# How the row maxima of a softmax are turned: by blocks on VectorE, or on TensorE at another place

## The chip, the cores and the metric

The kernel runs on one core of one Trainium2 chip. The metric is the device time of one execution in microseconds. Five engines work beside each other: TensorE (PE in the profile, with its weight loads as PEld), VectorE (DVE), ScalarE (ACT), GpSimd (POOL) and SyncE (SP), which here only issues DMAs.

## What is computed

One transformer block on 2048 rows of width 512: a modulated layer norm, attention with 32 heads of width 16, an output projection, a second modulated norm and a gated feed-forward of width 1792. The part around the change is the softmax of the attention:

```python
qkv = (x @ wqkv).reshape(B, S, 3, H, Dh).transpose(2, 0, 3, 1, 4)
q, k, v = qkv[0], qkv[1], qkv[2]
scores = jnp.einsum("bhqd,bhkd->bhqk", q, k) * Dh ** -0.5
p = _softmax(scores, axis=-1)
o = jnp.einsum("bhqk,bhkd->bhqd", p, v)
```

All of it is in fp32; products that need more than one pass of the narrower type split an operand into a high and a low part.

## The kernel before

**Units and steps.** The attention is cut into 32 units: 4 chunks of 512 queries by 8 groups of 4 heads. A unit has 16 steps (one per 128 keys), a step has four pairs (one per head). A pair is two matmuls that share the array, each on one half of its rows: the score of this step (`score`, L506, keys by queries, followed on ACT by the exponential, L508), and one product for the row maximum of a later unit (`max_one`, L479, queries by keys, followed on DVE by a reduce over 512 keys, L481). The maxima run some 20 steps ahead of the scores (`LEAD` = 21). The value products (`pv_step`, L521) use all 128 rows and 32 columns a head; they come in halves of a step.

**Where the maxima go.** The scores are computed with keys on the partitions, so the maximum of a query must be subtracted along the free axis. It is therefore appended to the queries as two more rows (`KR` = 48, and the next) of the operand `qop`, the high part of -max and the remainder, against two rows of ones in the keys. But the maxima lie with queries on the partitions, 128 x 16 values for a unit. `max_rows` (L483) reduces the four parts of each maximum on DVE (L486), negates them on ACT (L498), and turns them on TensorE by three products with a unit matrix (L491 to L493): the high part into one row, the remainder into the other. ACT copies the result out (L495), and two DMAs on SP put it into `qop` (L497).

**The order.** It is written by hand. `after(i)` runs behind step i and starts `max_rows` for unit u behind step 16u-6. `max_rows` does its reduce at once and puts five small jobs into `side`; `pair_of` takes one of them behind each pair. The third is the negation, the fifth is the turn on TensorE with its copy and DMAs. So the turn stands among the pairs.

**Plain and filled steps.** In `plain` three pairs are followed by one or two halves of value products (`HALVES`), and that is all TensorE does; four banks of the accumulator take maxima in turn, three take scores. In `filled` two steps (eight pairs) form a group: between the pairs stand matmuls of the projection or the feed-forward of the chunk before (L719, "filler", up to three yields of two matmuls behind a pair), and behind the eighth pair come `hook` (the DVE work of the filler that has ended) and four halves of value products. Three banks take maxima, two take scores. Filler of a gate-up job takes two groups, that of a down job one. The first filled step is 147, 275 or 403 (`STARTS`); the steps of a chunk are 8 filled, 12 plain (36 in the last), then filled for gate-up and down jobs, with 3 plain ones near the end. The maxima end 20 steps before the scores do; the filled groups behind that point have scores alone, with another order of banks (`ALONE`).

Of the kernel before, what the change touches and what calls it, by code (L numbers as in the profile page):

```python
# [9 lines left out]
F32 = mybir.dt.float32  # L10
F32R = mybir.dt.float32r
# [3 lines left out]
ALU = mybir.AluOpType  # L15
AX = mybir.AxisListType
# [3 lines left out]
P = 128  # L20
# [18 lines left out]
KR = 48  # L39
# [62 lines left out]
def block_kernel(ctx, tc, x, wqkv, wo, w_gate, w_up, w_down, c, w_mod, out):  # L102
    nc = tc.nc
# [18 lines left out]
    four, bank, single = Turn(0, 1, 2, 3), Turn(4, 5, 6), Turn(7)  # L122
# [326 lines left out]
    pb = ctx.enter_context(tc.tile_pool(name="pb", bufs=2, reuse_waits="tile"))  # L449
# [33 lines left out]
    def max_rows(u):  # L483

        m = pb.tile([P, 16], F32, name="m", tag="m")
        nc.vector.tensor_reduce(m, mx.pop(u).rearrange("p b s t f -> p (b s t) f"), op=ALU.max, axis=AX.X)  # L486
        nm = pb.tile([P, 16], F32R, name="nm", tag="nm")

        def rows():
            pr = bank("pr")[0:16, 0:2 * P]  # L490
            nc.tensor.matmul(pr[:, 0:P], nm.bitcast(F32), ident, start=True, stop=True)  # L491
            nc.tensor.matmul(pr[:, P:2 * P], m, minus, start=True, stop=False)  # L492
            nc.tensor.matmul(pr[:, P:2 * P], nm.bitcast(F32), minus, start=False, stop=True)  # L493
            mr = pb.tile([16, 2, P], F32R, name="mr", tag="mr", bufs=1)
            nc.scalar.copy(mr, pr.rearrange("p (r q) -> p r q", r=2))  # L495
            for r in range(2):
                nc.sync.dma_start(qop[u][KR + r:KR + r + 65:64].bitcast(F32), mr[:, r, :].bitcast(F32))  # L497
        side.extend([lambda: None, lambda: None, lambda: nc.scalar.mul(nm, m, -1.0), lambda: None, rows])  # L498

    def score(i, h):  # L500
        u, kt = divmod(i, 16)
# [73 lines left out]
    def split_weights():  # L575

        def raw(src, k):
            t = tile_mid().bitcast(F32)
            nc.gpsimd.dma_start(t.rearrange("p e c -> p (e c)").rearrange("p (k c) -> p k c", k=k), src)
            return t  # L580

        def parts(hi, lo, t):
            nc.gpsimd.tensor_copy(hi, t)
            nc.gpsimd.tensor_sub(lo, t, hi.bitcast(F32))

        def store(dst, w):
            nc.gpsimd.dma_start(dst, w.bitcast(F32))

        def cols(m):
            return slice(m * FG * P, (m + 1) * FG * P)  # L590

        srcs = [(wod[:, 2 * k:2 * k + 2, :], 2) for k in range(NK // 2)]
        for m in range(NF // FG):
            srcs += [(wgd[:, :, cols(m)], NK), (wud[:, :, cols(m)], NK), (wdd[:, m * FG:(m + 1) * FG, :], FG)]
        ahead = [raw(*srcs.pop(0)) for _ in range(2)]
        yield

        def following():
            if srcs:
                ahead.append(raw(*srcs.pop(0)))  # L600
            return ahead.pop(0)

        for k in range(NK // 2):
            t = following()
            nc.gpsimd.tensor_mul(t, t, ga_bc[:, None, :].to_broadcast([P, 2, D]))
            w = tile_gu()
            parts(as_wo(w)[:, 0], as_wo(w)[:, 1], t)
            store(wo_dr[k], as_wo(w))
            yield
        for m in range(NF // FG):  # L610
            ws = [tile_gu() for _ in range(FG)]
            for e in range(2):
                t = following()
                src = t.rearrange("p e c -> p (e c)").rearrange("p (k f c) -> p f k c", k=NK, f=FG)
                for f in range(FG):
                    parts(ws[f][:, 2 * e], ws[f][:, 2 * e + 1], src[:, f])
                    if e:
                        store(gu_dr[m * FG + f], ws[f])
                yield
            t = following()  # L620
            nc.gpsimd.tensor_mul(t, t, gb_bc[:, None, :].to_broadcast([P, FG, D]))
            w = tile_wd()
            parts(w[:, 0], w[:, 1], t)
            store(wd_dr[m], w)
            yield

    class Chunk:
# [42 lines left out]
        def rows(self, t):  # L670
            return self.nt[t // 2][:, t % 2, :]
# [139 lines left out]
    side = []  # L811
# [53 lines left out]
    at(UG - 2, lambda: chunks[0].load_wo())  # L865

    weights2 = split_weights()

    def after(i):
        nonlocal pf  # L870
        for f in due.pop(i, []):
            f()
        j = i + LEAD
        if j % 16 == 15 and j < n:
            max_rows(j // 16)
        if i == -2:
            run(late)
            sm.finish()
            es_a0.close()
            pf = ctx.enter_context(tc.tile_pool(name="pf", bufs=1, side="right", reuse_waits="tile"))  # L880
            kop[2] = pf.tile([P, 2, S], F32R, name="kop2")
            ones_rows(2)
            load_k(2)
            load_q(2)
        if 0 <= i < UG and i % 16 in (3, 5, 8):
            next(weights2, None)

    for i in range(-LEAD, -1):
# [7 lines left out]
        while side:  # L896
            side.pop(0)()

    halves = [(i, half) for i in range(n) for half in range(2)]
    done, ended, owed = 0, 0, 0  # L900
    three = Turn(0, 1, 2)
# [12 lines left out]
    def pvs(most, by_halves):  # L914

        nonlocal owed
        if by_halves:
            most, owed = most + owed, 0
        while most and halves and 4 * halves[0][0] + 8 <= done:
            i, half = halves.pop(0)  # L920
            pv_step(i, half)
            most -= 1
            if i % 16 == 15 and half:
                close_unit(i // 16, done // 4 - 1)
                if by_halves:
                    break
        if by_halves and most and halves and 4 * halves[0][0] + 8 <= done:
            owed = most

    def end_steps():  # L930
        nonlocal ended
        while ended < done // 4:
            after(ended - 1)
            ended += 1

    def plain(steps, tails=()):

        nonlocal four, bank
        assert steps % WIN == 0 and done % 4 == 0
        four, bank = Turn(0, 1, 2, 3), Turn(4, 5, 6)  # L940
        for w in range(4 * steps // WIN):
            for _ in range(WIN):
                pair_of()
            if w >= 4 * steps // WIN - len(tails):
                tails[w - 4 * steps // WIN](four())
            pvs((HALVES[(w - 2) % 4] if done > 8 else 0) + (w == 4 * steps // WIN - 1), True)
            end_steps()

    def filled(places, work):

        nonlocal four, bank
        four, bank = three, Turn(4, 5)
        if done >= 4 * n - 4 * (LEAD - 1):
            places, bank = ALONE.get(places, places), Turn(4, 5, 0, 1, 5, 0, 4, 1)
        for r in range(len(places)):
            pair_of()
            take(work, places[r])
            if r % 4 == 3:
                end_steps()
        hook()  # L960
        pvs(6, False)

    def two_of(u):
        return [kop[u % 3][:, e, :].rearrange("p (k c) -> p k c", k=NK) for e in range(2)]
# [102 lines left out]
```

## Time and profile before

| | |
|---|---|
| time, median of 3 runs | 1880.32 us (1879.69 to 1880.54) |
| span of the profiled execution, first to last instruction | 1875.6 us |
| median less span | 4.7 us |
| PE busy | 1846.7 us, 98% of the span |
| DVE busy | 1541.8 us, 82% |
| ACT busy | 1252.4 us, 67% |
| POOL busy | 415.3 us, 22% |
| granted TensorE clock, mean | 0.999 |

The span belongs to one execution on which the profiler was on; what that execution took beside its span is not listed, so times of whole runs are compared with times of whole runs. Busy times of PE are not its load: matmuls are pipelined, and one that waits behind another in the array counts as busy. In a row of a group the two numbers behind the bar are the busy time of the group (us) and the mean duration of one instruction (ns), then the idle time of the engine just before them and what ended it. In the timeline the columns are the start and the duration in us, engine, line, operation, names, shapes and count, with an idle time before the instruction in brackets. In the table of windows each engine has its busy time and, in brackets, its number of instructions, in the order PE, PEld, DVE, ACT, POOL, and then the granted clock, the DMA share and the GB/s.

### The profile page before, as it was taken

Reading aid. Unit: us, or ns where it says so; the run is one execution under the profiler, and the core shown is the slowest. Engines: PE = TensorE matmul, PEld = TensorE weight load, DVE = VectorE, ACT = ScalarE, POOL = GpSimd, SP = SyncE. Lnnn points to the kernel's source line nnn. Section 1 sums busy time; section 2 is a strip of 40 time slices with the busy share of each in tenths; the row PEclk is TensorE's granted clock in tenths of the full one; section 3 lists DMA queues with packets and bytes.
Section 4 is the critical chain, followed back from the end, with each engine's and each line's share of the span. In section 5 each row is a group of like instructions: output and inputs, shape, how many; then the busy total and the mean of one; then the engine's idle time right before and its main releaser. Section 6 shows DMA issues by size and latency. Waiting matters only on the chain.

```text
span 1875.6 us, 41002 instructions
## 1 busy us (share of the span) xinstructions
PE 1846.7 (98%) x16996; PEld 1160.4 (62%) x16996; DVE 1541.8 (82%) x2558; ACT 1252.4 (67%) x2406; POOL 415.3 (22%) x498
## 2 busy tenths in 40 slices
PE   7999999999999999999999999999999999999999
PEld 5766444444455766666555667666554566667887
DVE  5548999999999888888999888889999988831643
ACT  4221888888887766777777776677878877674211
POOL 3000454456323211111133111111123011030200
PEclk9999999999999999999999999999999999999999
DMA  8855677766843534554454454453643446243642
GB/s 286 292 198 142 174 183 178 201 167 190 211 86 78 145 102 124 144 124 90 107 124 116 108 127 131 121 122 78 159 86 56 108 92 156 86 159 119 249 180 110
DMA packets 78854, 267.62 MB, mean 143 GB/s; under 512 B 17364, under 2 KB 22484, under 8 KB 57988
## 3 DMA queue, kind: packets, MB, share of 16 engines
q1 hardware_dynamic: 59820, 180.10, 33.0%
q0 software_dynamic: 18160, 84.10, 19.0%
q8 instruction: 133, 2.18, 0.5%
q10 hardware_dynamic: 688, 0.80, 0.1%
q14 instruction: 53, 0.43, 0.1%
HBM read 201.85 MB, written 62.13 MB: 141 GB/s over the span
## 4 chain that ended last, share of the span: by engine, by line
PE 95%; DVE 2%; ACT 2%; DMA 0%; issue 0%; SPq 0%; ACTq 0%; DVEq 0%
PE bank L521 26%; PE bank L506 22%; PE bank L719 19%; PE bank L479 10%; PE bank L729 7%; PE bank L209 7%; DVE mx L481 1%; PE bank L762 1%; PE bank L491 1%; PE bank L162 0%; PE bank L703 0%; DMA wm_ab<-in_w_mod 0%; DVE stt L745 0%; PE bank L279 0%; PE bank L493 0%; PE bank L492 0%
## 5 line engine op out<-in xcount | busy, mean ns | idle before, releaser
L481 DVE TENSOR_REDUCE mx<-bank 128x1 f32<-128x512 f32 x2048 | 1286.5, 682 | 119.5 <-PE bank L479 72.4
L479 PE MATMUL bank<-kop,qop 48*128 48x512 f32 x2048 | 748.0, 432 | 3.6 <-DVE mx L481 3.4
L506 PE MATMUL bank<-qop,kop 50*128 50x512 f32 x2048 | 742.1, 427 | 4.6 <-ACT pt__20499 L508 0.5
L506 PEld LDWEIGHTS bank<-qop,kop 50*128 50x128 f32 x2048 | 347.0, 184 | 305.6 <-issue 63.3
L479 PEld LDWEIGHTS bank<-kop,qop 48*128 48x128 f32 x2048 | 343.9, 184 | 30.7 <-DVE mx L481 14.4
L719 PE MATMUL bank<-act,wgu 64*128 64x512 f32 x1872 | 297.9, 392 | 0.0
L719 PEld LDWEIGHTS bank<-act,wgu 64*128 64x128 f32 x1872 | 188.4, 187 | 30.9 <-DVE m L779 0.3
L548 POOL TENSOR_TENSOR on<-o,rb 128x512 f32<-128x512 f32 x31 | 39.7, 1282 | 442.9 <-DMA rb<-d_dr 304.0
L719 PE MATMUL bank<-wd,mid 64*128 64x512 f32 x912 | 136.5, 397 | 0.0
L781 POOL CAST mid<-m 128x512 fp32r<-128x512 f32 x40 | 24.3, 609 | 430.1 <-PE bank L479 165.5
L719 PEld LDWEIGHTS bank<-wd,mid 64*128 64x128 f32 x912 | 93.3, 185 | 12.0 <-issue 0.8
L209 PE MATMUL bank<-hT,wqs 128*128 128x512 f32 x384 | 95.7, 399 | 2.1 <-DVE prt L369 0.8
L209 PEld LDWEIGHTS bank<-hT,wqs 128*128 128x128 f32 x384 | 70.3, 188 | 24.3 <-issue 6.1
L777 DVE SCALAR_TENSOR_TENSOR q<-th,bank 128x512 f32<-128x512 f32 x56 | 37.7, 673 | 57.4 <-ACT th L773 57.2
L773 ACT ACTIVATE th<-bank 128x512 f32<-128x512 f32 x56 | 33.2, 593 | 58.3 <-PE bank L729 57.9
L793 DVE TENSOR_TENSOR x<-bank,x 128x512 f32<-128x512 f32 x84 | 53.8, 684 | 20.4 <-PE bank L506 20.2
L369 DVE TENSOR_TENSOR prt<-bank,prt 128x512 fp32r<-128x512 f32 x32 | 22.0, 688 | 46.5 <-ACT prt L367 46.5
L367 ACT CAST prt<-bank 128x512 fp32r<-128x512 f32 x32 | 18.8, 587 | 60.2 <-PE bank L209 46.9
L779 DVE TENSOR_TENSOR m<-bank,q 128x512 f32<-128x512 f32 x56 | 38.7, 691 | 21.2 <-PE bank L729 19.1
L729 PE MATMUL bank<-wd,mid 128*128 128x512 f32 x216 | 52.1, 394 | 0.4 <-DVE mid L782 0.3
L782 POOL TENSOR_TENSOR mid<-m,mid 128x512 fp32r<-128x512 f32 x40 | 51.6, 1291 | 3.3
L719 PE MATMUL bank<-wgu,act 64*128 64x512 f32 x288 | 47.7, 394 | 0.1
(6282 smaller groups left out, 5155.0 us busy)
## 6 DMA issues: line engine op xcount, KB each, us to landing
wgu<-gu_dr SPq DMA_DIRECT2D x48, 1024.0 KB
wd<-wd_dr SPq DMA_DIRECT2D x28, 1024.0 KB
kop<-kd SPq DMA_DIRECT2D x33, 768.0 KB
kop<-kd POOLq DMA_DIRECT2D x29, 768.0 KB, 8.5
gu_dr<-wgu POOLq DMA_DIRECT2D x14, 1024.0 KB, 14.1
kd<-prt SPq DMA_DIRECT2D x16, 512.0 KB
qd<-prt SPq DMA_DIRECT2D x16, 512.0 KB
kop<-gu_dr SPq DMA_DIRECT2D x8, 1024.0 KB
```

The costliest lines, as they stand in the source:

```text
L209: nc.tensor.matmul(pt, lhs(a, k), rhs(b, k), start=(n == 0), stop=(n == 3 * nk - 1))
L479: nc.tensor.matmul(pm, qop[u][rows, s, qt * P:(qt + 1) * P], kop[u % 3][rows, s, kc * CW:(kc + 1) * CW], start=True, stop=True)
L481: nc.vector.tensor_reduce(mx[u][:, b, s, qt, kc:kc + 1], pm, op=ALU.max, axis=AX.X)
L506: nc.tensor.matmul(sp, kop[u % 3][rows, h // 2, kt * P:(kt + 1) * P], qop[u][rows, h // 2, :], start=True, stop=True)
L521: nc.tensor.matmul(pv[u][32 * h:32 * h + 32, cols], v_flat[:, e0:e0 + 32], p_[h][:, cols], start=(kt == 0 and half == 0), stop=(kt == 15), ...
L548: mul.tensor_mul(on, o, rb)
L719: nc.tensor.matmul(outs[e], lhs(e, a, k)[rows], rhs(b, k)[rows], start=(ph == 0 and j == 0), stop=(j == z and (ph == 1 or trade is not None)),
L729: nc.tensor.matmul(outs[e], lhs(e, a, k), rhs(b, k), start=(j == 0), stop=(j == z))
L777: nc.vector.scalar_tensor_tensor(q, th, 1.0, outs[0], op0=ALU.add, op1=ALU.mult)
L779: nc.vector.tensor_mul(m32, outs[1], q)
L782: (nc.gpsimd if slow else nc.vector).tensor_sub(mid[:, 1, :], m32, mid[:, 0, :].bitcast(F32))
L793: nc.vector.tensor_add(ch.x2[:, t, :], outs[e], ch.x2[:, t, :])
```

## The change

A second way of turning is added, `max_turned`. It reduces as before, negates on ACT as the second small job, and as the fourth it runs two operations on DVE: the remainder (-max less its high part), and a transpose of the 128 x 32 tile in blocks of 32 x 32, which leaves each quarter of a row of 128 queries on a group of partitions of its own. The fifth job issues eight DMAs on SP in place of two, each with sixteen pieces of 32 queries. No TensorE instruction and no ACT copy is left. It is used for maxima that are complete in filled steps (`beside`).

Maxima that are complete in plain steps still go through `max_rows`, but once the main loop runs (`started`) the fifth job only notes the turn in `behind`, and it is done behind the value products of that group of pairs, in front of `end_steps`. Unit 0, which is done before the main loop, stays as it is.

```diff
-        side.extend([lambda: None, lambda: None, lambda: nc.scalar.mul(nm, m, -1.0), lambda: None, rows])
+        side.extend([lambda: None, lambda: None, lambda: nc.scalar.mul(nm, m, -1.0), lambda: None,
+                     (lambda: behind.append(rows)) if started else rows])
+
+    def max_turned(u):
+
+        m = pb.tile([P, 16], F32, name="m", tag="m")
+        nc.vector.tensor_reduce(m, mx.pop(u).rearrange("p b s t f -> p (b s t) f"), op=ALU.max, axis=AX.X)
+        parts = pb.tile([P, 2, 16], F32R, name="parts", tag="parts", bufs=1)
+        turned = pb.tile([P, 32], F32, name="turned", tag="turned", bufs=1)
+
+        def blocks():
+            nc.vector.scalar_tensor_tensor(parts[:, 1], m, -1.0, parts[:, 0].bitcast(F32), op0=ALU.mult,
+                                           op1=ALU.subtract)
+            nc.vector.transpose(turned, parts.rearrange("p r j -> p (r j)").bitcast(F32))
+
+        def rows():
+            for r in range(2):
+                for p in range(4):
+                    dst = qop[u][KR + r:KR + r + 65:64].bitcast(F32).rearrange("b s (t q) -> b (s t) q", t=4)
+                    j = 32 * p + 16 * r
+                    nc.sync.dma_start(dst[:, :, 32 * p:32 * p + 32], turned[j:j + 16])
+        side.extend([lambda: None, lambda: nc.scalar.mul(parts[:, 0], m, -1.0), lambda: None, blocks, rows])
...
-            max_rows(j // 16)
+            (max_turned if beside else max_rows)(j // 16)
...
+    def turn_behind():
+        while behind:
+            behind.pop(0)()
+
     def plain(steps, tails=()):
-        nonlocal four, bank
+        nonlocal four, bank, beside
+        beside = False
...
             pvs((HALVES[(w - 2) % 4] if done > 8 else 0) + (w == 4 * steps // WIN - 1), True)
+            turn_behind()
             end_steps()
...
     def filled(places, work):
-        nonlocal four, bank
+        nonlocal four, bank, beside
+        beside = True
...
         hook()
         pvs(6, False)
+        turn_behind()
```

More of the change, by code (lines that the diff above doesn't have):

```diff
@@ L867, in block_kernel @@
     weights2 = split_weights()
+    beside, started, behind = False, False, []
     def after(i):
@@ L897, in block_kernel @@
             side.pop(0)()
+    started = True
     halves = [(i, half) for i in range(n) for half in range(2)]
```

## The prediction

> **What bounds the kernel now.** I read the page first: who ends last, and the heaviest DVE group.
>
> ```profile
> PE 95%; DVE 2%; ACT 2%; DMA 0%; issue 0%; SPq 0%; ACTq 0%; DVEq 0%
> ...
> L481 DVE TENSOR_REDUCE mx<-bank 128x1 f32<-128x512 f32 x2048 | 1286.5, 682 | 119.5 <-PE bank L479 72.4
> ```
>
> The chain is PE nearly everywhere, but that is an average over two kinds of stage. The table of windows separates them: a stretch of plain steps, then one of filled steps.
>
> ```profile
> 300.00:336.00 36.00, 36.00 (x368) 16.74 (x366) 35.80 (x62) 31.60 (x62) 19.14 (x20) 1.00 0.77 197
> 690.00:740.00 50.00, 50.00 (x540) 34.59 (x540) 44.94 (x72) 35.57 (x70) 8.74 (x10) 1.00 0.48 115
> ```
>
> PE looks full in both. DVE (third pair of numbers) is at 35.80 of 36 in the plain stretch and at 44.94 of 50 in the filled one. So **plain steps go at DVE's pace**, PE being held by banks that DVE has not yet read, and **filled steps go at PE's pace**. The granted clock is 1.00 in both.
>
> Now the turn itself, by line: 64 records for 32 units, two per product, three products, so six records.
>
> ```profile
> L491 PE MATMUL bank<-ident,nm x64: 272/278/283, 177.4 to 1653.9; 128*16 128x128 f32 x64
> ```
>
> What it costs a filled group is read from the starts of the value products in the chain: they open the tail of each group, so the distance between two of them is one group.
>
> ```profile
> 676.29 1.86 PE bank L521 x32
> 683.06 1.87 PE bank L521 x32
> 690.75 1.87 PE bank L521 x32
> 697.61 1.86 PE bank L521 x32
> ...
> 738.63 1.86 PE bank L521 x32
> 746.50 1.87 PE bank L521 x32
> ...
> 780.52 1.86 PE bank L521 x32
> 787.46 1.86 PE bank L521 x32
> ...
> 899.26 1.87 PE bank L521 x32
> 907.50 1.87 PE bank L521 x32
> ```
>
> 683.06 to 690.75 holds the turn of unit 12: 7.69 us, against 6.77 before it and 6.86 behind it. 738.63 to 746.50 holds unit 13's, in a group of a down job: 7.87, against 6.94 for such a group without one (780.52 to 787.46). 899.26 to 907.50 is unit 16's, among the pairs of a down group: 8.24.
>
> **The change, filled steps.** From the code, unit u's maxima are complete behind step 16u-6, and that decides which path it takes: 1 to 10, 17, 18 and 25 to 28 fall to plain steps (16 units), 11 to 16, 19 to 24 and 29 to 31 to filled ones (15); unit 0 is done earlier and stays.
>
> PE loses six records and both passages around them. Nine units (11, 12, 14, 15, 19, 20, 22, 23, 30) lie as unit 12: 7.69 - (6.77 + 6.86)/2 = 0.87 each, 7.8 us. Three (13, 21, 29) lie as unit 13: 7.87 - 6.94 = 0.93, 2.8 us. Two (16, 24) as unit 16: 8.24 - 6.94 = 1.30, 2.6 us. Unit 31 stands alone, in groups that have no maxima any more:
>
> ```profile
> 1651.55 1.86 PE bank L521 x32
> 1658.84 1.86 PE bank L521 x32
> ...
> 1672.31 1.86 PE bank L521 x32
> 1678.15 1.86 PE bank L521 x32
> ```
>
> 7.29 with the turn, 5.84 without: 1.4 us (the turn also takes one bank out of a rotation written for eight calls). Filled sum: 7.8 + 2.8 + 2.6 + 1.4 = **14.6 us off PE**, provided that PE stays the bound.
>
> What is added must then be hidden. DVE gets two small operations, the 128x16 remainder and the 128x32 turn by blocks. The trace shows neither. From the nearest rows each is bounded between the smallest DVE operation of that kind and a small one on 16 columns:
>
> ```profile
> L682 DVE SCALAR_TENSOR_TENSOR rs<-rs 128x4 f32<-128x4 f32 x3 | 0.5, 163 | 0.1
> L536 DVE RECIPROCAL dn<-dn 128x16 f32<-128x16 f32 x32 | 7.7, 241 | 6.9 <-DMA dn<-o 6.9
> L486 DVE TENSOR_REDUCE m<-mx 128x16 f32<-128x64 f32 x32 | 6.9, 215 | 0.9
> L793 DVE TENSOR_TENSOR x<-bank,x 128x512 f32<-128x512 f32 x84 | 53.8, 684 | 20.4 <-PE bank L506 20.2
> ```
>
> So 0.33 to 0.48 us together; I take 0.45, the row with the same 16 columns being the nearer. If the block turn cost as much as a whole reduce of 512 columns (682 ns above), 0.9 together. They are queued behind the last maximum of the group, and that is where DVE idles:
>
> ```profile
> 682.00 1.92 DVE L481 TENSOR_REDUCE mx<-bank 128x1 f32<-128x512 f32 x3
> 685.42 0.69 DVE L481 TENSOR_REDUCE mx<-bank 128x1 f32<-128x512 f32 x1 [1.50 <-PE bank L479]
> ```
>
> DVE waits 1.50 us for the value products to end, so 0.45 or 0.9 costs nothing. In unit 13's group two additions of the down job (the 684 row) stand there too, and the next maximum comes perhaps 0.2 us late; with three banks in rotation PE is not held by that. If the cover were gone, 15 x 0.45 = 6.8 us would come back. ACT loses the copy of the turned rows and does the negation one pair earlier, where a pair's exp leaves it idle as well; nothing there.
>
> SP issues eight DMAs in place of two, each of a quarter row:
>
> ```profile
> L497 SPq DMA_DIRECT2D qop<-mr x64: 525/536/555, 178.7 to 1655.6; - x64
> L506 PEldq EVENT_SEMAPHORE  x33: 51/51/51, 186.9 to 1660.9; - x33
> ```
>
> At 0.54 us with a little between, an estimate of 0.6 each, eight take 4.8 us. They no longer wait for PE's turn in the next group: DVE has the blocks at about 684.4 (682.00 + 1.92 + 0.45), the last piece is issued by 689.2. The unit's first score is the fifth pair behind the tail that starts at 690.75, so near 694 once 0.87 is gone. What SP holds behind them (weights, the key and query loads of the next unit) finds SP free again within 5 us and is loaded a job ahead. PE must wait for more DMA signals at the unit's first score, a few more of these 51 ns; its queue runs ahead of the array, so nothing, at worst 0.2 us x 15 = 3 us, which I keep for the range.
>
> The Trainium skill, DMA: Bandwidth & Descriptors, Specifications, gives 512 B as the least transfer for line rate and says that below it the engine reads, modifies and writes; the pieces here fall from 512 to 128 B. That speaks against the change, and no run here shows its price; 8 KB per unit with some 5 us of room leaves the sum as it is, unless the slow rival below holds.
>
> **The change, plain steps.** PE keeps the turn, and DVE sets the pace, so only DVE's idle time counts. Unit 5, two pairs, turn, third pair, value products of one half:
>
> ```profile
> 377.15 0.39 PE L506 MATMUL bank<-qop,kop 50*128 50x512 f32 x1
> 377.47 0.39 PE L491 MATMUL bank<-ident,nm 128*16 128x128 f32 x2
> ...
> 378.23 0.50 PE L506 MATMUL bank<-qop,kop 50*128 50x512 f32 x1
> ...
> 378.66 0.40 PE L521 MATMUL bank<-pt__3775,v_flat 128*32 128x256 f32 x1
> ...
> 379.23 0.49 PE L506 MATMUL bank<-qop,kop 50*128 50x512 f32 x1
> ...
> 379.56 0.39 PE L506 MATMUL bank<-qop,kop 50*128 50x512 f32 x1
> ...
> 379.80 0.39 PE L506 MATMUL bank<-qop,kop 50*128 50x512 f32 x1
> 380.12 0.40 PE L521 MATMUL bank<-pt__3775,v_flat 128*32 128x256 f32 x1
> ```
>
> Pair to pair takes 0.24, pair to value products 0.32, one half of them 0.57 to the next pair, and from the turn's start to the next pair 0.76 (377.47 to 378.23). Moved, unit 5 runs: third pair 377.39, products 377.71, turn, next group's pair at 377.71 + 0.57 + 0.76 = 379.04, if products-to-turn costs what products-to-pair does. That is 0.19 earlier than 379.23. The Trainium skill, TensorEngine Tiling (Array Packing), Key Properties, says that a change of tiling mode drains TensorE; the 0.32 against 0.24 above agrees with it, and by it the moved turn, whose neighbours use all 128 rows as it does, might be another 0.1 us cheaper in each plain unit; the trace has no such passage, and the sum does without it.
>
> Unit 4 goes the other way, for two halves follow its turn:
>
> ```profile
> 337.65 0.50 PE L506 MATMUL bank<-qop,kop 50*128 50x512 f32 x1
> ...
> 338.08 0.40 PE L521 MATMUL bank<-pt__3248,v_flat 128*32 128x256 f32 x1
> ...
> 339.08 0.50 PE L506 MATMUL bank<-qop,kop 50*128 50x512 f32 x1
> ```
>
> ```profile
> 335.74 3.67 DVE L481 TENSOR_REDUCE mx<-bank 128x1 f32<-128x512 f32 x6
> 339.65 1.88 DVE L481 TENSOR_REDUCE mx<-bank 128x1 f32<-128x512 f32 x3 [0.25 <-PE bank L479]
> ```
>
> Its third pair needs a bank that the second of these six maxima frees, at 335.74 + 0.60 + 0.68 = 337.0 (0.60 is their pitch); so it starts at some 337.2 and part of the turn fills a wait that is there anyway. Moved: products at 337.55, two halves 1.00 (338.08 to 339.08), turn 0.76, next pair at 339.31 in place of 339.08. DVE idles 0.25 now and would idle 0.48.
>
> By the halves in the group list, six units (2, 5, 8, 10, 18, 26) are like 5: -0.19 each, -1.1. Four (1, 4, 7, 28) are like 4: +0.23, +0.9. In the other six the third pair also waits a little for its bank, gain and loss cancel: 0. **Plain sum: -0.2 us**, with bounds of +0.3 and -0.25 for each of 16 units, +5 and -4.
>
> **Sum.** 14.6 + 0.2 = 14.8 us off the span of 1875.6: 1860.8. The median of the runs, 1880.32, is 4.7 above that span (that execution's own time beyond its span is not shown, so I take the 4.7 as what lies around it): 1865.5 us, 0.8% faster.
>
> **Rivals.** (1) *DVE becomes the bound in the groups that lose the turn.* For: in the window of a down group it has eight maxima (8 x 0.60), two additions (1.37), the reduce of the maxima (0.22) and 0.45, which make 6.84 of a 6.94 us group. Against: 1.50 us idle in unit 12's. If a third of the 14.6 is lost so: 1870.5. Chance 0.15. (2) *The moved turn starves DVE in every plain unit*, as in unit 4: 16 x 0.25 = +4, that is 1869.5. For: products and turn then stand in one stretch without a pair. Against: unit 5's working. 0.12. (3) *The rows come late, slower than before.* Place: SP, between the block turn and the unit's first score. The eight pieces have from 684.4 to about 694, 1.2 us each where 0.54 is measured for an issue of four times as long pieces. From 1.2 us on every unit stalls PE by eight times the excess, and the 14.6 is used up at 1.3 to 1.4 us (8 x 0.12 x 15 = 14.4). At 1.5 us each: 15 x 8 x 0.3 = 36 us lost against 14.8 gained, 1901 us. Against: SP is idle there, and 8 KB is nothing. 0.04. (4) *It doesn't do what it says*: the choice is made when the maxima are complete, so units near an edge may take the other path; even with four more units on PE, 4 x 0.93: 1869. 0.05; and small losses everywhere that leave no difference, 0.04. My forecast has the remaining 0.60.
>
> The range reaches from the plain bound on the good side (-4, rounded to 1862) to rivals 1, 2 and 4 with PE's added waits: **1862 to 1873**. This kernel's measurement can tell about 0.2% (3.8 us) from no change: faster 0.91 (forecast, rivals 1, 2, 4, less a little), same 0.04, slower 0.05.
>
> **What would show it.** Right: groups with a filled unit's block turn last 6.8 (7.0 for down), L491 to L493 have 34 records each in place of 64, no PE wait on qop's DMAs, DVE's two new operations inside the idle at the value products. Plain: units 1, 4, 7, 28 with a DVE idle near 0.5, those like 5 near 0.1. Wrong: PE held by L481 behind the new operations, a first score waiting for DMA, or block turns far over 0.25 us. The filled sum falls if the neighbours of a removed turn grow by what the turn cost.

## The result, and the profile after

The changed kernel takes **1865.34 us** (median of 6 executions, 1861.2 to 1872.57) against 1880.43 (6 executions, 1879.23 to 1886.2) for the one before on the same chip: a ratio of 0.9921, with a 95% interval of 0.9902 to 0.994. (Of all executions below, one of the plain part alone took 2465.34 us at a mean clock of 0.656, and its ratio leaves that one out.) The forecast was 1865.5. To be met within 0.2 us is luck: the plain part gave 2 us more than forecast, the sum took 2.9 us too much for what lies around the span, and late transfers and half-clock stretches took about as much back as these two together, as the sections below show.

The page of the kernel after: the chain, and the row of the maxima.

```profile
PE 94%; DMA 2%; DVE 2%; ACT 1%; SPq 0%; issue 0%; ACTq 0%; DVEq 0%
...
L481 DVE TENSOR_REDUCE mx<-bank 128x1 f32<-128x512 f32 x2048 | 1283.0, 681 | 104.9 <-PE bank L479 67.8
```

PE is the bound as before. The table of windows for the same two stretches, plain and filled (the columns as before):

```profile
300.00:336.00 36.00, 36.00 (x364) 16.86 (x360) 35.87 (x62) 31.85 (x63) 17.03 (x18) 1.00 0.77 195
690.00:740.00 50.00, 50.00 (x524) 35.21 (x522) 44.83 (x74) 35.61 (x72) 7.79 (x9) 1.00 0.48 115
```

DVE is still full in the plain stretch (35.87 of 36) and has the same 5 us to spare in the filled one. So neither stage has changed its bound; what changed is how much PE has to do in a filled group. The value products in the chain of the kernel after (lines have moved: value products L521 are now L542, scores L506 are L527, filler L719 is L740):

```profile
679.89 1.86 PE bank L542 x32
...
686.68 1.86 PE bank L542 x32
...
693.55 1.86 PE bank L542 x32
...
734.58 1.86 PE bank L542 x32
...
741.54 1.87 PE bank L542 x32
...
748.32 1.86 PE bank L542 x32
```

The group that held unit 12's turn now takes 686.68 - 679.89 = 6.79 us where it took 7.69, and unit 13's takes 741.54 - 734.58 = 6.96 where it took 7.87. The groups behind them, without a turn, take 6.87 and 6.78. The forecast had been 6.8, and 7.0 for a down group. Nothing that replaced the turn shows in PE's time.

What replaced it: on DVE, by the timeline of DVE around unit 12's block turn, and on SP, by its own timeline.

```profile
678.23 2.53 DVE L481 TENSOR_REDUCE mx<-bank 128x1 f32<-128x512 f32 x4
680.67 0.16 DVE L509 SCALAR_TENSOR_TENSOR parts<-m,parts 128x16 fp32r<-128x16 f32 x1
680.87 0.21 DVE L511 STREAM_TRANSPOSE turned<-parts 128x32 f32<-128x32 f32 x1
682.25 5.27 DVE L481 TENSOR_REDUCE mx<-bank 128x1 f32<-128x512 f32 x8 [1.17 <-PE bank L479]
```

```profile
681.11 4.38 SPq L518 DMA_DIRECT2D qop<-turned  x8
```

The two operations stand where DVE waits for the value products, and 1.17 us of that wait is left behind them. SP has issued the eight pieces at 685.49; the unit's first score starts at 690.94.

By line, over all 15 units on the new path, and the turn that PE keeps:

```profile
L509 DVE SCALAR_TENSOR_TENSOR parts<-m,parts x15: 161/165/175, 626.2 to 1636.1; 128x16 fp32r<-128x16 f32 x15
```

```profile
L511 DVE STREAM_TRANSPOSE turned<-parts x15: 211/212/213, 626.4 to 1636.5; 128x32 f32<-128x32 f32 x15
```

```profile
L491 PE MATMUL bank<-ident,nm x34: 272/273/283, 175.7 to 1476.8; 128*16 128x128 f32 x34
```

0.165 + 0.212 = 0.38 us on DVE (0.45 had been taken, bounds 0.33 to 0.48), 4.38 us on SP (0.55 a piece; 4.8 taken), and 34 records in place of 64, so 17 units on PE and 15 on the new path, as counted.

**Unit by unit.** To see where the time went I took the start of the 33rd score of every unit in both traces; the growth of the difference from one unit to the next is what that unit gained or lost (us, minus is faster). The last column is a second run of the same kernel, beside the experiments (called "the changed kernel, again" below).

| units | forecast, each | after | after, again |
|---|---|---|---|
| 11, 12, 14, 15, 19, 20, 22, 23, 30 | -0.87 | -0.84 to -0.97 | -0.83 to -0.94 |
| 13, 21, 29 | -0.93 | -0.86, -0.93, -0.87 | -0.90, -0.92, -0.90 |
| 16, 24 | -1.30 | -1.26, -1.26 | -1.20, -1.25 |
| 31 | -1.4 | -1.44 | -1.42 |
| **filled, sum** | **-14.6** | **-14.8** | **-14.8** |
| 2, 10, 26 (like 5) | -0.19 | -0.30, -0.28, -0.31 | -0.31, -0.26, -0.28 |
| 3, 9, 17, 25, 27 (like 6) | 0 | -0.13 to -0.19 | -0.07 to -0.16 |
| 1, 4, 7 (like 4); 28 | +0.23 | +0.06 to +0.10; -0.21 | +0.08, +0.09, +0.60; -0.21 |
| 5, 6, 8, 18 | (as above) | -0.31, -0.17, +0.55, +1.72 | +0.93, -0.15, +0.69, +0.10 |
| before unit 0 | 0 | -1.69 | -1.83 |
| behind unit 31's 33rd score (tail) | 0 | +6.21 | +1.65 |
| span | -14.8 | -10.2 | -14.4 |

The filled units do what was forecast, to 0.2 us in 14.6. (Unit 28's -0.21 comes with the filled part: it stays with the filled part alone, -0.26, and goes with the plain part alone, +0.05.) The rest of the table is of two kinds. Before unit 0 nothing was changed; a wait of PE for a weight (wm_ab) is 1.1 us shorter there in this execution. Units 8 and 18 and the tail lose by something else. In unit 8 DVE waits for a transfer of softmax denominators, by the timeline of DVE after; before, the same operation came with no wait:

```profile
512.96 0.25 DVE L557 RECIPROCAL dn<-dn 128x16 f32<-128x16 f32 x1 [0.77 <-DMA dn<-o]
```

In the tail ACT waits longer for the last output of the attention, first before, then after:

```profile
ACT kop L667 <- DMA kop<-o_dr: 16.1, 1, 16.1
```

```profile
ACT kop L688 <- DMA kop<-o_dr: 19.6, 1, 19.6
```

These are transfers that the change does not touch. And two stretches ran at half the clock, by the table of windows after:

```profile
983.60:990.50 6.90, 6.90 (x51) 3.14 (x45) 5.85 (x14) 2.98 (x8) 4.55 (x17) 0.51 0.01 2
...
1720.90:1724.30 3.40, 3.40 (x10) 2.63 (x9) 2.72 (x5) 1.11 (x2) 0.00 (x0) 0.50 0.00 0
```

The first is unit 18's +1.72, the second part of the tail's +6.21. Executions of this kernel differ by such stretches, though not by them alone, since the last two here have the same clock: the six have spans of 1859.4, 1860.0, 1861.7, 1865.4, 1865.8 and 1870.8 at mean clocks of 1.000, 0.999, 0.999, 0.997, 0.995 and 0.995. The Trainium skill, TensorE: Matmul & The Clock Gate, Part 1, gives 4/8 of the clock after at least one idle window of about 3.4 us, and the full clock again after at least one busy one. The lengths here, 3.4 and 6.9 us, agree; an idle window of 3.4 us does not show: in the 20 us ahead of the first stretch PE never stood for more than 0.31 us in one piece, ahead of the second for 1.59.

### The profile page after: what moved, and what is told of

It reads as the page before. It is cut to its first block, busy times and chain, and to the rows that moved or that the text cites. A ratio compares the mean times of both kernels' runs of the same rounds, so it can differ in the third digit from the quotient of the medians.

```text
span 1865.4 us, 41049 instructions
## 1 busy us (share of the span) xinstructions
PE 1837.1 (98%) x16906; PEld 1157.4 (62%) x16906; DVE 1542.1 (83%) x2588; ACT 1244.7 (67%) x2391; POOL 415.3 (22%) x498
## 4 chain that ended last, share of the span: by engine, by line
PE 94%; DMA 2%; DVE 2%; ACT 1%; SPq 0%; issue 0%; ACTq 0%; DVEq 0%
PE bank L542 27%; PE bank L527 22%; PE bank L740 19%; PE bank L479 10%; PE bank L750 7%; PE bank L209 6%; DVE mx L481 1%; DMA dn<-o 1%; PE bank L162 0%; PE bank L724 0%; DMA kop<-o_dr 0%; DMA wm_ab<-in_w_mod 0%; DVE stt L766 0%; PE bank L279 0%; DMA rb<-d_dr 0%; DMA kd<-prt 0%
## 5 line engine op out<-in xcount | busy, mean ns | idle before, releaser
L527 PE MATMUL bank<-qop,kop 50*128 50x512 f32 x2048 | 737.3, 427 | 4.6 <-ACT pt__20559 L529 0.5
L527 PEld LDWEIGHTS bank<-qop,kop 50*128 50x128 f32 x2048 | 346.0, 184 | 304.6 <-issue 57.1
L740 PE MATMUL bank<-act,wgu 64*128 64x512 f32 x1872 | 296.8, 392 | 0.0
L740 PEld LDWEIGHTS bank<-act,wgu 64*128 64x128 f32 x1872 | 187.2, 187 | 30.5 <-issue 0.2
L740 PE MATMUL bank<-wd,mid 64*128 64x512 f32 x912 | 137.0, 397 | 0.0
L740 PEld LDWEIGHTS bank<-wd,mid 64*128 64x128 f32 x912 | 94.0, 185 | 11.7 <-ACT first L837 0.8
L740 PE MATMUL bank<-wgu,act 64*128 64x512 f32 x288 | 47.7, 394 | 0.1
```

What stands on the lines that cost most here:

```text
L527: nc.tensor.matmul(sp, kop[u % 3][rows, h // 2, kt * P:(kt + 1) * P], qop[u][rows, h // 2, :], start=True, stop=True)
L740: nc.tensor.matmul(outs[e], lhs(e, a, k)[rows], rhs(b, k)[rows], start=(ph == 0 and j == 0), stop=(j == z and (ph == 1 or trade is not None)),
```

## The experiments

Each was timed beside the kernel before on the same chip; ratios are to that kernel, with 95% intervals. Differences by unit are taken as in the table above, against the kernel before, or against the changed kernel's second run where that kernel is named. Where a kernel adds work that nobody reads, its section says so.

**The theory** was that of the prediction: in filled steps PE is the bound, the turn with its two passages is off it, and DVE and SP have room. Against it stood: (B) the gain is of the moved turn in plain steps; (C) it is a better place, not a shorter PE, that helps; (D) DVE or SP is close to being the bound.

### The changed kernel, again

> The changed kernel once more, for a trace to set beside the others. Its first trace has two dips of the granted clock and a late DMA in the tail that the trace of before has not. Theory A (the gain is the PE time of the turn in the 15 filled units, some 0.9 us each, and little else): at a clock of 1.000 the span is 1859 to 1861 us, each filled unit gains 0.85 to 1.0 us, units 16 and 24 1.3, unit 31 1.4. Theory B (a good part comes from the moved turn in plain steps): plain units show more than 0.4 us each.

1863.39 us against 1881.25: 0.9906 (0.9894 to 0.9919). The units are in the table. The filled ones come out within 0.1 us of the first run, one by one, so -14.8 is a property of the kernel; what units 5, 7, 8, 18 and the tail show is not.

### Filled part alone

```diff
-                     (lambda: behind.append(rows)) if started else rows])
+                     rows])
```

> Only the block turn in filled steps; in plain steps TensorE turns among the pairs as before. Theory A: nearly the whole gain, a span some 14.5 to 15 us under the one before and 0 to 3 us over the changed kernel. Theory B: half of the gain or less, 7 us or more over the changed kernel.

1865.89 against 1881.25: 0.9919 (0.9907 to 0.9932); the interval overlaps that with both parts, and the medians differ by 2.5 us, about what the plain part gives by units (next section). Filled units -0.83 to -0.97, -1.20, -1.24 and -1.42. Units 1 to 10 run the instructions of the kernel before, and yet units 6, 8 and 10 come out 0.93, 0.65 and 0.37 later than before. In 6 and 8 DVE waits 0.85 and 0.56 us for denominators, in 10 there is a stretch at half the clock: that is the size of what varies by itself.

### Plain part alone

```diff
-                     (lambda: behind.append(rows)) if started else rows])
+                     (lambda: behind.append(rows)) if started and not beside else rows])
...
-            (max_turned if beside else max_rows)(j // 16)
+            max_rows(j // 16)
```

> Only the move in plain steps; in filled steps TensorE turns among the pairs as before. Theory A: 0 to 3 us under the kernel before (the prediction's working gives 0.2; the first trace of the changed kernel suggests 0.2 to 0.3 in units like 5 and 6, nothing in units like 4). Theory B: 7 us or more under it.

1879.39 against 1881.25: 0.9992 (0.9983 to 1.0001), so by whole times alone it is not told from no change. Filled units within 0.08 of before. Plain ones: like 5, -0.15 to -0.34 (unit 5 itself +0.58, since DVE waits 0.79 us there for denominators); like 6, -0.13 to -0.18; like 4, +0.05 to +0.10. Without unit 5 they add up to -1.9, and with the -0.31 that unit 5 gains in the next run, which moves the turn in plain units in the same way, to -2.2, where the forecast had -0.2 for all. So (B) is refuted as the source: the plain part is about an eighth of the gain. Most of the excess over the forecast has the size of one passage, which the timeline of PE shows in the changed kernel, unit 5 (the last value products, the turn, the next pair, the next value products and the pair behind them):

```profile
375.96 0.38 PE L542 MATMUL bank<-pt__3802,v_flat 128*32 128x256 f32 x1
376.15 0.38 PE L491 MATMUL bank<-ident,nm 128*16 128x128 f32 x2
...
376.59 0.38 PE L493 MATMUL bank<-minus,nm 128*16 128x128 f32 x2
376.90 0.50 PE L527 MATMUL bank<-qop,kop 50*128 50x512 f32 x1
...
378.12 0.38 PE L542 MATMUL bank<-pt__3802,v_flat 128*32 128x256 f32 x1
378.42 0.50 PE L527 MATMUL bank<-qop,kop 50*128 50x512 f32 x1
```

Value products to pair: 378.12 to 378.42, 0.30 (0.309 is the median of 439 such passages). Value products to turn: 375.96 to 376.15, 0.19 (0.196 is the median of 16). The forecast used the first for the second. The Trainium skill, TensorEngine Tiling (Array Packing), Key Properties, says that a change of tiling mode drains TensorE; the trace agrees in so far as the passage from 128 rows to 50 and 48 takes 0.11 us more, and it shows no such price from 128 rows by 32 columns to 128 by 16. 0.11 us in 16 units is 1.8 us.

### PE's turn behind the value products everywhere

```diff
+        if beside:
+            side.extend([lambda: None, lambda: nc.scalar.mul(nm, m, -1.0), lambda: None, lambda: behind.append(rows)])
+            return
...
-            (max_turned if beside else max_rows)(j // 16)
+            max_rows(j // 16)
```

> TensorE turns everywhere, and everywhere behind the value products, in filled steps too (there the negation stands one pair and the turn two pairs earlier than before, so that it falls behind the same group's value products). Theory A (what counts in filled steps is that the turn leaves PE): a filled unit still pays 0.56 us of products and 0.1 of passage, so 0.2 to 0.3 us are gained in each, 3 to 4.5 us, and with the plain part 4 to 7 us under the kernel before, 9 or more over the changed one. Rival C (what costs is the place among the row halves): within 3 us of the changed kernel.

1881.85 against 1879.68: 1.0012 (1.0003 to 1.0022). I had expected a few us of gain, and the filled units lost 0.17 to 0.29 each instead, all but 16, 24 and 31 (-0.07, -0.31, -0.27). The waits of PE, and the chain around unit 12:

```profile
PE bank L530 <- ACT mr L495: 6.8, 15, 0.5
```

```profile
682.40 1.86 PE bank L545 x32
...
684.94 0.37 ACT mr L495
...
690.35 1.86 PE bank L545 x32
```

7.95 us where the kernel before took 7.69. The turn took an accumulator bank that the next score also wanted, and PE stood 0.45 us in each of 15 units until ACT had copied the result out. Take those 0.45 away and the place gains some 0.2 a unit, about what the cheaper passages are worth; this is a subtraction, no run has the place without the stall. By it (C) is refuted with a margin: a better place for the turn on PE is worth 0.2 us a unit, leaving PE 0.9.

### Block turns in all units

```diff
-            (max_turned if beside else max_rows)(j // 16)
+            (max_turned if started else max_rows)(j // 16)
```

> The block turn in all units of the main loop, TensorE turns only unit 0. Theory A: in plain steps DVE sets the pace, so its 0.38 us for two operations comes on top in each of 16 units, less the idle time that the PE turn leaves there (0 in units like 5, 0.36 in units like 4): 3 to 5 us over the changed kernel. Rival D (TensorE's turn is the dearer one everywhere): 2 us or more under the changed kernel.

1904.45 against 1879.68: 1.0158 (1.0113 to 1.0204), some 40 us over the changed kernel by the medians (34 by the profiled spans) where a few had been expected. Against the changed kernel, units 9, 17 and 27 cost 0.1 to 0.2, which would be DVE's 0.38 in a DVE-bound stage less PE's turn; units 10, 18 and 26 about 1; units 2, 4 and 5 cost 5.8, 4.5 and 7.3, units 7 and 8 some 3. Five of the 34 us lie before unit 0, where nothing was changed, and stretches at half the clock are part of the rest. Two things come together. The rows are late, by the waits of PE:

```profile
PE bank L527 <- DMA qop<-turned: 6.2, 4, 2.5
PE bank L527 <- issue: 3.8, 1, 3.8
```

A plain group is shorter than a filled one: from the last piece's issue to the unit's first score there are 3.0 to 5.7 us in the filled units, and 1.13 to 1.44 in 12 of the 16 plain ones, so the rows land at most 1.13 us behind the last issue's end, and PE waits there. And DVE's first operation is held, by up to 1.8 us: the run with the two DVE operations in plain steps, below, shows that by itself.

### The block turn five and thirteen times

Work that nobody reads is added: the same block turn, repeated.

```diff
-            nc.vector.transpose(turned, parts.rearrange("p r j -> p (r j)").bitcast(F32))
+            for _ in range(13):
+                nc.vector.transpose(turned, parts.rearrange("p r j -> p (r j)").bitcast(F32))
```

> The changed kernel with the block turn done five times over, 0.85 us more on DVE in each filled unit. Theory A (hidden in the idle time of 1.17 us at the value products): within 1.5 us of the changed kernel. If DVE were near its bound in filled steps: 12 us over it.

> The block turn thirteen times over, 2.5 us more on DVE in each filled unit, 1.4 us beyond the idle time. Theory A: maxima run late by 1.4 us, PE is held by a bank some pairs later, 0.4 to 1.0 us in each unit, 6 to 15 us over the changed kernel. If DVE had still more room: no difference.

Five: 1865.59 against 1879.68, 0.9936 (0.9912 to 0.9959). Thirteen: 1894.42, 1.0084 (1.006 to 1.0109). Five add about 1.0 us of DVE per unit (four times 3.17/13, the row below): units like 12 lose nothing (-0.03 to +0.09 over the changed kernel), 13, 21 and 29 lose 0.3 to 0.4, and 16 and 24 lose 0.6 and 1.0. Thirteen add 2.9: units like 12 lose 1.2, 13, 21 and 29 lose 2.3 to 3.8, 16 and 24 lose 4 (more than was added, part of it at half the clock). The timeline of DVE and the waits of PE, at thirteen:

```profile
684.57 3.17 DVE L512 STREAM_TRANSPOSE turned<-parts 128x32 f32<-128x32 f32 x13
```

```profile
PE bank L479 <- DVE mx L481: 16.0, 18, 2.1
```

So a gate-up group hides 2.9 - 1.2 = 1.7 us more than it has to (1.17 of it is the idle time in the timeline above; the rest may be what the three banks buffer, which no run separates), and a down group, whose two additions already stand there, 1.0 - 0.4 = 0.6. Of (D), DVE is refuted at the true price, 0.38, and its threshold is known.

### The pieces issued twice and three times

Unread work again: each DMA of L518 is repeated, to the same place.

```diff
-                    nc.sync.dma_start(dst[:, :, 32 * p:32 * p + 32], turned[j:j + 16])
+                    for _ in range(2):
+                        nc.sync.dma_start(dst[:, :, 32 * p:32 * p + 32], turned[j:j + 16])
```

> The changed kernel with each of the eight DMAs issued twice: sixteen of 0.54 us, 8.7 us on SP for a filled unit, the last landing some 0.9 us later. The units have 9.8 us from the block turn to the first score as unit 12, 9.0 as unit 13, 7.4 as units 16 and 24. Theory A: unit 12 and its like are just in time, units 13, 21, 29 late by 0 to 0.7 us, 16 and 24 by 2: 2 to 8 us over the changed kernel. If DMAs had far more room: no difference.

> Each of the eight DMAs three times: twenty-four, 13 us on SP. By the third rival's price the rows are late by 4 us in units like 12, 5 in those like 13, 6.5 in 16 and 24: 50 to 65 us over the changed kernel if PE stands still for all of it, less where maxima and filler go on; in any case slower than the kernel before.

2125.64 against 1879.81, 1.1307 (1.1287 to 1.1328), and 2311.79, 1.2295 (1.2268 to 1.2322). Far beyond what had been expected, and the fault is the experiment's. In the timeline of SP sixteen issues took

```profile
702.60 23.21 SPq L519 DMA_DIRECT2D qop<-turned  x16
```

23.2 us, not 16 x 0.54 = 8.6. The second write to a place starts 1.57 us (median) after the first and not 0.54, so it seems to wait until the first has landed (702.60, 704.20, then the next pair at 704.77), and once in each of 13 units an issue stands 7.4 to 9.0 us (713.19 to 721.12 here). The run shows that late rows stall PE in all 15 units (the row below), but it does not price a plain issue.

```profile
PE bank L528 <- DMA qop<-turned: 222.7, 15, 17.8
```

### Eight issues to a spare place ahead of the rows

The same question without that fault: eight small DMAs, which nobody reads, to their own places in DRAM, ahead of the eight.

```diff
+            for k in range(8):
+                nc.sync.dma_start(spare[u, k], turned[16 * k:16 * k + 16])
```

> The changed kernel with eight DMAs of the same blocks into spare memory ahead of the eight real ones. It repeats the run with doubled DMAs without its fault, that a second write to a place waits for the first to land. SP takes 8.7 us for sixteen issues and the rows are there 1.24 us later (both measured); the room from the block turn to the first score is 9.8 us in units like 12, 9.0 in those like 13, 7.4 in 16 and 24. Theory A: late by 0.1, 0.9 and 2.5 us; with what a standing TensorE costs behind that in clock, 8 to 25 us over the changed kernel, near or over the kernel before. If the rows have more room than that: no difference.

1886.24 against 1879.3: 1.0036 (1.0023 to 1.005), slower than before, as expected. The timeline of SP around unit 13, and the waits of PE:

```profile
737.49 3.63 SPq L516 DMA_DIRECT2D spare<-turned  x8
741.16 4.38 SPq L521 DMA_DIRECT2D qop<-turned  x8
745.65 0.35 SPq L681 DMA_DIRECT2D wd<-wd_dr  x1
746.04 0.43 SPq L676 DMA_DIRECT2D wgu<-gu_dr  x1
```

```profile
PE bank L743 <- DMA wgu<-gu_dr: 9.3, 3, 3.9
PE bank L530 <- DMA qop<-turned: 4.6, 3, 2.2
```

Twice the time on SP costs 22 us over the changed kernel, and it goes by unit (of those on the new path): 12, 14, 15, 19, 20, 22, 23 and 30 lose at most 0.1, 31 loses 0.5, unit 11 loses 0.6, 13, 21 and 29 lose 3.4, 6.5 and 6.8, 16 and 24 lose 4.9 and 3.0. In 16 and 24 the rows are late (the waits are 2.2 and 1.5 us); in 13, 21 and 29 PE waits 2.5 to 3.9 us for weights, which are queued behind the rows on SP (745.65 and 746.04 here). In 16, 21, 24 and 29 a stretch of 3.4 to 6.8 us at half the clock follows and is part of the loss. Rival 3's mechanism is real, and twice the change's time on SP is already too much; where between once and twice the loss begins no run shows.

### The two DVE operations in plain steps too

PE turns as in the changed kernel, but DVE also does both new operations in plain units, unread.

```diff
-        nm = pb.tile([P, 16], F32R, name="nm", tag="nm")
+        parts = pb.tile([P, 2, 16], F32R, name="parts", tag="parts", bufs=1)
+        turned = pb.tile([P, 32], F32, name="turned", tag="turned", bufs=1)
+        nm = parts[:, 0]
+
+        def blocks():
...
-                     (lambda: behind.append(rows)) if started else rows])
+        side.extend([lambda: None, lambda: None, lambda: nc.scalar.mul(nm, m, -1.0),
+                     blocks if started else lambda: None,
```

> The changed kernel, and in plain steps the remainder and the block turn are done on DVE as well, with nobody reading them; TensorE still turns and SP still issues two DMAs. It prices DVE's two operations in plain steps without the late rows of the run that turned by blocks everywhere. Theory A (DVE sets the pace there): 0.3 to 0.38 us in each unit like 5 and 6, where DVE has no idle time left, 0 to 0.1 in units like 4, which have 0.36: 3 to 5 us over the changed kernel. If DVE had room in plain steps: nothing.

1871.34 against 1879.3: 0.9949 (0.9929 to 0.9968); some 6 to 8 us over the changed kernel. The execution with the trace is the slowest of the four (1880.44; the one with a mean clock of 1.000 took 1867.17), so the losses by unit are those of a bad case. Units 9, 10, 17, 25, 26 and 27 lose 0.03 to 0.41, but units 2, 4 and 6 lose 4.5, 5.9 and 3.6. The line of the first operation says why, and then two timelines, of DVE and of POOL, around units 2 and 6:

```profile
L492 DVE SCALAR_TENSOR_TENSOR parts<-m,parts x16: 158/346/2614, 220.8 to 1495.7; 128x16 fp32r<-128x16 f32 x16
```

```profile
261.03 1.78 DVE L492 SCALAR_TENSOR_TENSOR parts<-m,parts 128x16 fp32r<-128x16 f32 x1
...
427.70 2.32 DVE L492 SCALAR_TENSOR_TENSOR parts<-m,parts 128x16 fp32r<-128x16 f32 x1
```

```profile
260.38 2.39 POOL L650 TENSOR_TENSOR mid<-mid,gb_bc 128x1024 f32<-128x1024 f32 x1
...
427.59 2.39 POOL L650 TENSOR_TENSOR mid<-mid,gb_bc 128x1024 f32<-128x1024 f32 x1
```

An operation of 0.165 us takes 1.78 and 2.32. It ends at 262.81 and 430.02; GpSimd's operation ends at 262.77 and 429.98. In all eight cases where it took over 0.3 us, it ended 0.02 to 0.05 us behind the end of a GpSimd operation; in seven this was running when it began, in one (342.41) it is shown to begin 0.19 us later. So the remainder (two inputs from SBUF) appears to be held until GpSimd is through. It does not hold for every operation: three times (602.07, 1009.05 and 1416.61) it ran its 0.16 us inside a GpSimd TENSOR_SCALAR of 0.8 us. The Trainium skill, SBUF — State Buffer, Who interferes with whom, says that a DVE instruction with two SBUF inputs contends with a GpSimd one that reads SBUF, that the shared ports are an exclusive lock, and that the order of issue decides who is blocked; the eight cases agree, the three do not show it. In the first chunk GpSimd splits weights with operations of 1.04 to 2.4 us, so the block turn in plain steps would have met this; in filled steps the 15 take 161 to 175 ns, and no operation of GpSimd runs at that moment in the trace after. The maxima behind the held operation are then late and PE waits. In units 7 and 8, where the operation takes 2.08 and 2.14 us, that costs 1.1 each; in 2, 4 and 6 PE's clock is halved behind it for 3.4 to 10 us (from 265.2, 347.1 and 432.4), and they lose 3.6 to 5.9. The end times are observed; that the port is the reason is the page's, and it was not tried by moving GpSimd's work away.

### The remainder added on GpSimd, two products on PE

```diff
+        lo = pb.tile([P, 16], F32, name="lo", tag="lo")
...
-            nc.tensor.matmul(pr[:, P:2 * P], m, minus, start=True, stop=False)
-            nc.tensor.matmul(pr[:, P:2 * P], nm.bitcast(F32), minus, start=False, stop=True)
+            nc.tensor.matmul(pr[:, P:2 * P], lo, minus, start=True, stop=True)
...
+                     lambda: nc.gpsimd.tensor_add(lo, m, nm.bitcast(F32)),
```

> The changed kernel, and for units in plain steps the remainder is added up on GpSimd, so that TensorE turns with two products (four records) in place of three (six). PE saves 0.22 us in 17 units. Theory A (DVE sets the pace there, PE time counts only where DVE idles): units like 4 gain up to 0.2, those like 5 and 6 nothing, 0 to 1.5 us in all. If PE time counted in plain steps as well: 3.5 us.

1966.59 against 1881.25: 1.0453 (1.044 to 1.0467). It was to save one product, 0.22 us in each plain unit, and lost 3.4 to 9.9 us in 14 of the 16. The waits of PE:

```profile
PE bank L494 <- POOL lo L500: 72.4, 14, 7.2
```

The chain around unit 3's turn shows the queue that stands in front of that small addition:

```profile
313.80 2.37 POOL mid L644
...
316.22 1.04 POOL wd L606
...
317.34 2.35 POOL wd L607
...
320.58 0.24 POOL lo L500
...
320.87 0.61 PE bank L494 x2
```

GpSimd is busy 21% of the span, and still an operation of 0.24 us stood behind these 6 us of others, since the program has GpSimd split weights at that time and the chain shows it taking one after the other. A share of busy time says nothing about the wait of one operation.

## Why the prediction was right, step by step

**The bounds: right.** Plain steps went on at DVE's pace, filled ones at PE's. Nearly all of the gain is work that left PE in filled steps.

**The filled sum: right,** -14.8 measured against 14.6, in two runs and in the kernel with that part alone. The terms were distances between groups, with and without a turn, and not durations of the turn. The turn's three products alone are three starts of 0.22 us, 0.66; the other 0.2 are, by subtraction, the passages around them.

**The cover: right.** DVE's two operations cost 0.38 and nothing is lost by them; 1.17 us of cover is left in a gate-up group, and some 0.6 in a down group like unit 13's (turns five and thirteen times). In units 16 and 24 little is left: of the 1.0 us that five turns add, 16 loses 0.6 and 24 all. The eight issues took 4.38, and nothing waits for the rows.

**The plain sum: the size was wrong.** -0.2 was forecast, about -2.2 came. The mis-sized term is "0.57 + 0.76", where products to turn was put at the cost of products to pair: it costs 0.196, not 0.309, and 16 times the difference is 1.8. The text had given this 0.1 as a possibility, and the sum did without it. That it counts in full is argued, not shown: by the prediction's own rule only DVE's idle time counts in plain steps, and with the turn moved that falls in unit 5 from 0.28 to 0.02 us (it gains 0.31) but in unit 3 from 0.10 to 0.03 (it gains 0.15). Half of the gain in units like 6 stays open. The order of the classes was right (like 5 gains most, like 4 loses, and DVE idles 0.30 us at unit 4's turn, where 0.48 had been expected and 0.25 stood before).

**The 4.7 us around the span: wrong as a term.** Every execution listed takes about 1.8 us (1.7 to 2.0) more than its span (1867.15 and 1865.4; 1863.52 and 1861.7). The execution profiled before, with its span of 1875.6, therefore took about 1877.4, 3 us under the median: it was a quick one. The sum from there would be 1862.6, and with the better plain sum about 1860.6, which is near what the kernel does when the clock holds (spans of 1859.4 and 1860.0 give 1861.2 and 1861.7). The median lies some 4 above that because of late transfers and half-clock stretches, of which the kernel before has its own share. Adding the 4.7 put the forecast on the median by treating those as fixed cost.

**The rivals.** (1) DVE as the bound: not at 0.38; with thirteen turns it is. (2) The moved turn starves DVE in every plain unit: no, in the plain part alone only units 1, 4, 7 and 28 lose, 0.05 to 0.10 each. (3) Late rows: not here, but doubling SP's time makes the kernel slower than before. The threshold had been put at 1.2 us a piece for all units; from the last issue's end to unit 12's first score there are 5.45 us in the trace after, of which at most 1.13 are the landing, so eight pieces may take 0.54 more each: 1.1 us. In unit 16 it is 3.00, and the threshold 0.8. The run with the spare issues agrees: it shifts the rows by 3.9 us, units like 12 lose nothing, 16 and 24 do. What the rival's price lacked are the weights behind the rows on SP: with them late, units 13, 21 and 29 lose more than the late rows cost elsewhere. (4) It does not do what it says: refuted by 34 records.

**What stays open.** No version beat the changed kernel; the idle time left on DVE beside the turns of plain steps is 0.3 us in four units (1, 4, 7 and 28). Why the transfer of the denominators is late in one or two units of some executions, and which executions fall to half the clock, was not settled; these make its executions spread over 11 us.

## What to carry to other kernels

Price a removed piece of work by the distance between two marks of its stage, with and without it, and only in the stage where its engine is the bound: here 0.9 us a unit for 0.66 of products. What PE's time is worth in the other stage, where DVE sets the pace, no run prices cleanly. What takes its place must be checked for cover at the very moment it runs, on every queue it joins: the same two DVE operations were free beside filler, and cost up to 6 us, half-clock stretch included, in a unit where GpSimd was at work, and twice as many issues on a queue that looked idle made the kernel slower than before. And a single profiled span is one draw from a spread; compare it with its own execution's time, not with the median of others.

## What the runs showed of the hardware

- The passage from 128x32 value products to 128x16 turn products takes 0.196 us, that to pairs on 48 and 50 rows 0.309.
- A small DVE operation with two inputs from SBUF took up to 2.61 us in place of 0.165, and ended with the GpSimd operation beside it (eight cases; beside a TENSOR_SCALAR of 0.8 us, three times, it was not held).
- A DMA issue of sixteen pieces of 128 B takes 0.496 us on SP, against 0.536 for an issue of the two rows (512 B pieces); the rows have landed by 1.13 us behind the last issue's end, since first scores start as early as that in the kernel with block turns in all units. What 512 B pieces take to land no trace here shows, so a loss below 512 B, which the prediction cites from the Trainium skill, is neither shown nor refuted; at 8 KB a unit it cost no time.
- A short stand of PE can be followed by 3.4 to 10 us at half the clock: with DVE's operation stretched to 1.8 to 2.6 us PE stood for 1.0 to 1.6 us in one piece and three units lost 3.6 to 5.9 us with such a stretch; two, after stands of 0.9 and 1.3 us, lost 1.1 without.
